# Attention key blocks paired 1 with 2 and 0 with 3, values cast once, and the channel spectra copied on VectorE

## The chip, the cores and the metric

The kernel runs on one core of one Trainium2 chip. The metric is the device time of one execution in microseconds (us); lower is better. The core has a TensorE for matmuls (PE in the profile, with its weight loads as PEld), VectorE (DVE), ScalarE (ACT), GpSimd (POOL) and SyncE (SP). SP and POOL issue the DMAs here, and 16 DMA engines carry them out. SBUF has 128 rows (partitions). PSUM takes the matmuls' results in banks of 512 fp32 numbers a row.

## The reference

Two stages follow each other: attention with a sliding window of 128 keys and a linear distance bias, then a spectral mixing layer over its output.

```python
# q, k, v: (8 batches, 8 heads, 576 tokens, 64)
scores = scale * np.matmul(q, k.transpose(0, 1, 3, 2))
rel = pos[:, None] - pos[None, :]
bias = slopes[:, None, None] * (-np.abs(rel))[None, :, :]
mask = (rel >= 0) & (rel < window)            # window = 128
scores = np.where(mask, scores + bias[None], -1000000000.0)
attn = softmax(scores)                         # over keys
x = np.matmul(attn, v)                         # -> (8, 576, 512)
...
X = np.fft.rfft(x, axis=1)                     # the first 64 modes are kept
Yr = einsum('bmd,mde->bme', Xr, w_r) - einsum('bmd,mde->bme', Xi, w_i)
Yi = einsum('bmd,mde->bme', Xr, w_i) + einsum('bmd,mde->bme', Xi, w_r)
y = np.fft.irfft(Y, n=S, axis=1)
u = x + y
return u + np.maximum(u @ w_ch, 0.0)
```

The inputs are fp32: q, k and v are 9.4 MB each, w_r and w_i have 64 matrices of 512 x 512 each (67 MB each), and w_ch is 1 MB. The output is (8, 576, 512) in fp32.

## The kernel before

Attention works in 16 units, a unit being one batch and four heads. A unit's four heads are two head pairs (e = 0, 1) times two positions h. The 576 tokens are four full blocks of 128 (`FULL = 4`) and a tail of 64 (`TAIL`). Because the window is 128 keys, a block of keys only meets the queries of its own block and of the next.

The scores are computed transposed, keys on the rows. One score tile `sc` holds two key blocks: 64 rows (even or odd keys, the index j) of one block in rows 0 to 63 and 64 rows of the other in rows 64 to 127. Before the change, `pair` 0 is blocks 0 and 1 and `pair` 1 is blocks 2 and 3. There are four score tiles in a unit, t = 2 * pair + h. ScalarE turns each into `att` with an exponential (`exp`, L307). For pair 0 the bias and the window are applied behind it by a multiplication with a table on VectorE (`mask`, L318); for pair 1 they are added in PSUM ahead of the scores, as a matmul with the identity (L284).

`value` multiplies `att` with the values. Each row group of 64 has its own copy place in `vb`: the values of the lower rows stand in the left W = 66 columns, those of the upper rows in the right 66, and the rest is zero. So one matmul over all 128 rows writes 132 columns, two query tiles at once. The two columns beyond the 64 of the head hold ones, which gives the softmax sums. The tail's values are in a tile of their own, `vt`. `norm` divides by the sums (L359 and L360) and writes x in bf16. `cast` brings q, k and v from fp32 to bf16 on VectorE (for v in two instructions of 64 rows, L246, and one for the tail, L248), and then issues the load of the unit two further on, as the raw buffers are double.

For each batch, `spectrum` transforms x to 64 modes on TensorE (L381), and `channels` copies the result from PSUM into XC with two ScalarE instructions (L402 and L403), the second with the opposite sign. For the last batch the work is halved between ScalarE and VectorE. The result of `spectrum` is in the same PSUM place (tag tp) as the transposes of k and q.

The order of the work is written by hand: the list `STAGE` says for each stage which step of which unit is issued, and every engine carries out its instructions in that order. The loads of q, k and v go through SP's queue (L232, L212, L225), those of v for the last two units through POOL's. The weights of the mixing layer are loaded by POOL with a conversion to bf16 (`load_w`, L472). In attention they are paced: a small copy (`gate`, L565) waits for the k cast of two units ahead, and behind it one weight matrix is loaded. Behind attention come packs of two matrices (`load_packs`, L491), and TensorE multiplies each matrix with the spectra as it lands (L886). A last part computes the output from the spectra and x (L842) and stores it.

Of the kernel before, what the change touches and what calls it, by code (L numbers as in the profile page):

```python
# [20 lines left out]
P = 128  # L21
D = 64
# [8 lines left out]
TPP = 9  # L31

W = D + 2

NC = 24

# [70 lines left out]
class _Attention:  # L107


    def __init__(self, tc, ctx, q, k, v, consts, x, XC, raw):  # L110
        self.tc, self.nc = tc, tc.nc
        self.q, self.k, self.v = q, k, v
        self.ident, self.F, self.FT = consts
        self.x, self.XC = x, XC
        B, H, S, _ = q.shape
        self.S, self.NG = S, H // 4
        self.units = [(b, g) for b in range(B) for g in range(self.NG)]
        self.raw = raw
        end = ctx.enter_context(tc.tile_pool(name="aend", bufs=1))
        self.sums = ctx.enter_context(tc.tile_pool(name="asum", bufs=2))  # L120
        self.mid = ctx.enter_context(tc.tile_pool(name="amid", bufs=2))
        self.ps = ctx.enter_context(tc.tile_pool(name="aps", bufs=1, space=PSUM))
        fix = ctx.enter_context(tc.tile_pool(name="afix", bufs=1))
        self.table = fix.tile([P, H, 2, 2 * P], BF16, name="mask")
        self.bias = fix.tile([P, H, 2, 2 * P], BF16, name="bias")
        self.qkT = [fix.tile([P, 2, 2, (FULL + 1) * P], BF16, name=f"qkT{i}") for i in range(2)]
        at = (fix, end)
        self.att = [at[i].tile([P, FULL * 8 * P + 64], BF16, name=f"att{i}") for i in range(2)]
        self.vb = [at[i].tile([P, 2, 4, 2, 2 * W], BF16, name=f"vb{i}") for i in range(2)]
        self.vt = [end.tile([P, 4, 2, W], BF16, name=f"vt{i}") for i in range(2)]  # L130
        self.loaded, self.casted, self.open = {}, {}, {}

    def fixtures(self, i):
        nc = self.nc
        for t, tail in ((self.vb[i], self.vt[i]),):
            for half in range(2):
                row = slice(64 * half, 64 * half + 64)
                c0 = W * half
                nc.gpsimd.memset(t[row, :, :, :, W - c0 : 2 * W - c0], 0.0)
                nc.gpsimd.memset(t[row, :, :, :, c0 + D : c0 + W], 1.0)  # L140
            nc.gpsimd.memset(tail, 0.0)
            nc.gpsimd.memset(tail[64:96, :, :, D:], 1.0)
        nc.gpsimd.memset(self.att[i][:, FULL * 8 * P :], 1.0)

    def distances(self, pool):

        nc = self.nc
        key_i = pool.tile([P, 2, 2], I32)
        for half in range(2):
            nc.gpsimd.iota(key_i[64 * half : 64 * half + 64], [[1, 2], [-P, 2]], base=0,  # L150
                           channel_multiplier=2)
        key = pool.tile([P, 2, 2], FP32)
        nc.gpsimd.tensor_copy(key, key_i)
        self.near = [pool.tile([P, 2, 2 * P], BF16) for _ in range(2)]

        def window(out, half, c0, width, n):
            row = slice(64 * half, 64 * half + 64)
            sign = 1 - 2 * n
            nc.gpsimd.affine_select(
                out=out[row, :, c0 : c0 + width],  # L160
                in_=key[row, :, n].unsqueeze(-1).broadcast_to([64, 2, width]),
                compare_op=ALU.is_ge, fill=-float(2**20), base=-n,
                pattern=[[-sign, 2], [sign, width]], channel_multiplier=-2 * sign,
            )

        for half in range(2):
            for n in range(2):
                window(self.near[0], half, n * P, P, n)
        nc.gpsimd.tensor_copy(self.near[1][:64], self.near[0][:64])
        nc.gpsimd.tensor_copy(self.near[1][64:, :, : P + TAIL], self.near[0][64:, :, : P + TAIL])  # L170
        window(self.near[1], 1, P + TAIL, TAIL, 0)

    def slope(self, h):
        return 2.0 ** (-8.0 * (h + 1) / self.table.shape[1])
# [26 lines left out]
    def load(self, w, u):  # L201
# [5 lines left out]
        if w == "v":  # L207
            t = self.raw[w][:, u % 2]
            sv = self.v[b, hs]
            if u < len(self.units) - 2:  # L210
                for h in range(4):
                    nc.sync.dma_start(  # L212
                        out=t[:, :2, h],
                        in_=sv[h, : FULL * P].rearrange("(r p j) d -> p r (j d)", r=2, j=2),
                    )
                queue = nc.sync
            else:
                for r in range(2):
                    nc.gpsimd.dma_start(
                        out=t[:, r],  # L220
                        in_=sv[:, 2 * r * P : 2 * (r + 1) * P].rearrange(
                            "h (p j) d -> p h (j d)", j=2),
                    )
                queue = nc.gpsimd
            queue.dma_start(  # L225
                out=t[64:96, 2],
                in_=sv[:, FULL * P :].rearrange("h (p j) d -> p h (j d)", j=2),
# [10 lines left out]
    def cast(self, u, w):  # L238

        nc = self.nc  # L240
        src = self.loaded.pop((w, u))
        if w == "v":
            src = src.rearrange("p s h (j d) -> p s h j d", j=2)
            for half in range(2):
                row = slice(64 * half, 64 * half + 64)
                nc.vector.tensor_copy(  # L246
                    self.vb[u % 2][row, :, :, :, W * half : W * half + D], src[row, :2])
            nc.vector.tensor_copy(self.vt[u % 2][64:96, :, :, :D], src[64:96, 2])  # L248
        else:
            dst = self.mid.tile([P, TPP, 2, D], BF16, tag=w, name=w)  # L250
            nc.vector.tensor_copy(dst.rearrange("p j e d -> p e j d"), src)
            self.casted[u, w] = dst
        self.load(w, u + 2)
# [20 lines left out]
    def score(self, u, t):  # L274
# [12 lines left out]
                )  # L287
        for j in range(2):
            for half in range(2):
                blk = 2 * pair + half  # L290
                spans = [(blk * P, 0, min(2 * P, self.S - blk * P))]
                if blk == FULL - 1:
                    spans.append((FULL * P, 192, TAIL))
                for k0, c0, n in spans:
                    for e in range(2):
                        row = slice(64 * e, 64 * e + 64)
                        nc.tensor.matmul(  # L297
                            sc[64 * half : 64 * half + 64, e, j * 256 + c0 : j * 256 + c0 + n],
                            lhsT=qkT[row, 1, h, k0 + j : k0 + P : 2],
                            rhs=qkT[row, 0, h, k0 : k0 + n],  # L300
                            start=not biased, stop=True, skip_group_check=biased,
                        )
        self.open[t, u] = sc
# [16 lines left out]
    def value(self, u, e):  # L320
# [1 line left out]

        nc = self.nc
        b, g = self.units[u]
        odd = b % 2
        att, vb, vt = self.att[u % 2], self.vb[u % 2], self.vt[u % 2]
        last = u == len(self.units) - 1 and e == 1
        av = self.ps.tile([P, 2, 512], FP32, tag="sc" if last else "av", bufs=2 if last else 1)
        for h in range(2):
            bank = av[:, h, : (FULL + 1) * W]  # L330
            todo = []
            for pair in range(2):
                rhs = [vb[:, pair, 2 * e + h, j] for j in range(2)]
                todo.append((pair, 0, 2 * pair, rhs))
                if pair == 1 and odd:
                    todo.append((pair, P, 3, [r[:, :W] for r in rhs]))
                    todo.append((pair, P - 64, 4, [r[:, W:] for r in rhs]))
                else:
                    todo.append((pair, P, 2 * pair + 1, rhs))
            todo.append((1, 192 - 64 * odd, 4, [vt[:, 2 * e + h, j] for j in range(2)]))  # L340
            for n, (pair, c0, qt, rhs) in enumerate(todo):
                for j in range(2):
                    o = (((2 * pair + h) * 2 + e) * 2 + j) * 256 + c0
                    nc.tensor.matmul(  # L344
                        bank[:, qt * W : qt * W + rhs[j].shape[1]],
                        lhsT=att[:, o : o + P], rhs=rhs[j],
                        start=(n == 0 and j == 0), stop=(n == len(todo) - 1 and j == 1),
                        skip_group_check=True,
                    )
        self.open["av", e, u] = av  # L350

    def norm(self, u, e):
# [2 lines left out]
        av = self.open.pop(("av", e, u))  # L355
        cs = slice((4 * g + 2 * e) * D, (4 * g + 2 * e + 2) * D)
        rec = self.sums.tile([P, 2, FULL + 1], FP32, tag="rec", name="rec")
        tiles = av[:, :, : (FULL + 1) * W].rearrange("p h (t n) -> p h t n", n=W)
        nc.vector.reciprocal(rec, tiles[:, :, :, D])  # L359
        nc.vector.tensor_tensor(  # L360
            out=self.x[:, b, :, cs].rearrange("p t (h d) -> p h t d", h=2),
# [28 lines left out]
    def channels(self, u, _):  # L390
# [8 lines left out]
            "p (q s t b m) -> p q t s b m", q=2, s=3, t=2, b=8)[:, :, :, :, b]  # L399
        if u < len(self.units) - 1:  # L400
            src = xt[:, 0].rearrange("p (q t) r m -> p q t r m", q=2)
            nc.scalar.copy(view[:, :, :, 1:], src)  # L402
            nc.scalar.mul(view[:, :, :, 0], src[:, :, :, 1], -1.0)  # L403
        else:
            lo, hi = slice(0, 2), slice(2, 4)
            nc.scalar.copy(view[:, 0, :, 1:], xt[:, 0, lo])
# [622 lines left out]
```

## Time and profile before

| | |
|---|---|
| median of the runs | 438.14 us (438.12 to 438.55, 3 runs) |
| the profiled execution | 437.99 us, of which the span of the profile is 436.1 us |
| granted TensorE clock, mean | 0.862 |
| busy in the span | PE 316.2, PEld 177.7, DVE 184.5, ACT 162.3, POOL 90.2 us |
| read from HBM, written to it | 162.53 MB, 9.44 MB |
| moved by the DMA engines | 105.54 MB, mean 242 GB/s |

How to read the profile: the page gives the busy time of each engine, then the span in 40 slices (a digit is tenths of the slice, PEclk the granted TensorE clock in tenths). "DMA share" is the time that packets were under way against 16 engines; it passes 1 where packets overlap on an engine. GB/s counts what is written: a weight that is read in fp32 and written in bf16 counts with half of what is read. The chain of waits is the work that ended last, followed back from the last instruction. A group of instructions has line, engine, operation, tiles and shapes, count, busy time and mean, and then the idle time before it with what ended it. A wait has the engine and line that waited, what it waited for, and the total, the number and the longest, in us.

### The profile page before, as it was taken

Reading aid. Unit: us, or ns where it says so; the run is one execution under the profiler, and the core shown is the slowest. Engines: PE = TensorE matmul, PEld = TensorE weight load, DVE = VectorE, ACT = ScalarE, POOL = GpSimd, SP = SyncE. Lnnn points to the kernel's source line nnn. Section 1 sums busy time; section 2 is a strip of 40 time slices with the busy share of each in tenths; the row PEclk is TensorE's granted clock in tenths of the full one; section 3 lists DMA queues with packets and bytes.
Section 4 is the critical chain, followed back from the end, with each engine's and each line's share of the span. In section 5 each row is a group of like instructions: output and inputs, shape, how many; then the busy total and the mean of one; then the engine's idle time right before and its main releaser. Section 6 shows DMA issues by size and latency. Waiting matters only on the chain.

```text
span 436.1 us, 8292 instructions
## 1 busy us (share of the span) xinstructions
PE 316.2 (73%) x3488; PEld 177.7 (41%) x3509; DVE 184.5 (42%) x332; ACT 162.3 (37%) x211; POOL 90.2 (21%) x170
## 2 busy tenths in 40 slices
PE   5589899979686635543442487999889999788982
PEld 4367677757565312111111133444434444334430
DVE  7789799887783301000000021322213233122684
ACT  6949899988681000000000011322222322102780
POOL 8701010103424002222112110101111110012600
PEclk9969999999999955555555569999999999989997
DMA  8999999999999999999999999999999999998598
GB/s 285 326 311 310 290 316 300 307 298 299 252 217 212 215 215 213 214 214 214 215 212 214 214 215 214 215 214 215 215 214 214 215 215 215 213 215 153 190 378 311
DMA packets 50453, 105.54 MB, mean 242 GB/s; under 512 B 4032, under 2 KB 21072, under 8 KB 50416
## 3 DMA queue, kind: packets, MB, share of 16 engines
q0 software_dynamic: 19440, 68.41, 77.9%
q1 hardware_dynamic: 30976, 36.60, 25.3%
q8 instruction: 27, 0.44, 0.4%
q14 instruction: 10, 0.08, 0.1%
HBM read 162.53 MB, written 9.44 MB: 394 GB/s over the span
## 4 chain that ended last, share of the span: by engine, by line
DMA 71%; PE 10%; DVE 8%; issue 5%; POOL 2%; ACT 1%; SPq 1%; DVEq 0%; POOLq 0%; ACTq 0%
DMA w<-in_moe_w_i_dram 42%; DMA wch<-in_moe_w_ch_dram 8%; DMA qr<-in_q_dram 7%; DMA vr<-in_v_dram 6%; DVE o L842 3%; DMA qr<-in_moe_w_i_dram 3%; PE my L702 2%; DMA vr<-in_moe_w_r_dram 2%; DMA kr<-in_k_dram 2%; DVE vb L246 1%; PE acc L886 1%; PE av L344 1%; POOL Z L648 1%; PE my L659 1%; DVE att L318 1%
## 5 line engine op out<-in xcount | busy, mean ns | idle before, releaser
L886 PE MATMUL acc<-w,XC 128*32 128x512 bf16 x456 | 80.3, 478 | 68.5 <-DMA w<-in_moe_w_i_dram 34.2
L886 PEld LDWEIGHTS <-XC 128*32 128x32 bf16 x508 | 38.4, 147 | 109.2 <-issue 82.8
L307 ACT ACTIVATE att<-sc 128x1024 bf16<-128x1024 f32 x64 | 64.1, 1032 | 9.7 <-PE sc L297 9.6
L636 ACT CAST ZW<-zw 128x512 bf16<-128x512 f32 x8 | 4.7, 585 | 142.9 <-PE zw L634 142.9
L344 PE MATMUL av<-vb,att 128*128 128x132 bf16 (+1 forms) x576 | 38.4, 217 | 13.3 <-DVE x L360 8.6
L344 PEld LDWEIGHTS <-att 128*128 128x128 bf16 x704 | 36.6, 98 | 18.7 <-DVE x L360 12.0
L608 DVE TENSOR_SCALAR yq<-acc 128x512 bf16<-128x512 f32 x14 | 9.6, 687 | 81.8 <-PE acc L886 81.8
L702 PE MATMUL my<-wch,xT 128*64 128x512 bf16 x288 | 34.5, 381 | 5.7 <-ACT x L733 4.2
L711 ACT CAST XW<-my 128x512 bf16<-128x512 f32 x36 | 19.3, 589 | 50.5 <-PE my L659 50.5
L683 DVE COPY xT<-tr 128x1024 bf16<-128x1024 bf16 x18 | 12.4, 692 | 54.9 <-PE tr L681 54.9
L269 ACT COPY qkT<-tp 128x1152 bf16<-128x1152 bf16 x30 | 33.5, 1116 | 4.1 <-PE tp L263 3.6
L491 POOL DMA_DIRECT2D w<-in_moe_w_r_dram x22 | 15.6, 710 | 72.1 <-PE acc L886 46.1
L491 POOL DMA_DIRECT2D w<-in_moe_w_i_dram x23 | 16.3, 709 | 64.1 <-PE acc L886 45.3
L297 PE MATMUL sc<-qkT 64*64 64x256 bf16 (+2 forms) x640 | 25.1, 263 | 4.8 <-ACT qkT L269 1.2
L360 DVE TENSOR_TENSOR x<-av,rec 128x640 bf16<-128x640 f32 x32 | 26.4, 825 | 1.1
L702 PEld LDWEIGHTS <-xT 128*64 128x64 bf16 x288 | 17.1, 109 | 21.5 <-issue 9.1
L246 DVE CAST vb<-vr 64x1024 bf16<-64x1024 f32 x32 | 22.6, 708 | 0.2
L733 ACT CAST x<-my 128x512 bf16<-128x512 f32 x18 | 10.5, 585 | 31.6 <-PE my L659 31.6
L297 PEld LDWEIGHTS <-qkT 64*64 64x64 bf16 x640 | 14.5, 109 | 19.1 <-issue 16.0
L734 DVE CAST x<-my 128x512 bf16<-128x512 f32 x18 | 12.4, 692 | 21.7 <-PE my L659 21.7
L842 DVE TENSOR_TENSOR o<-yy,r 128x1024 f32<-128x1024 f32 (+1 forms) x20 | 20.3, 1059 | 2.1 <-ACT r L802 1.9
L318 DVE TENSOR_TENSOR att<-att,mask 128x1024 bf16<-128x1024 bf16 x32 | 20.5, 682 | 0.0
(137 smaller groups left out, 424.7 us busy)
## 6 DMA issues: line engine op xcount, KB each, us to landing
w<-in_moe_w_i_dram POOLq DMA_DIRECT2D x23, 1024.0 KB, 36.2
w<-in_moe_w_r_dram POOLq DMA_DIRECT2D x22, 1024.0 KB, 35.6
qr<-in_q_dram SPq DMA_DIRECT2D x16, 576.0 KB, 7.9
kr<-in_k_dram SPq DMA_DIRECT2D x16, 576.0 KB, 7.9
w<-in_moe_w_r_dram POOLq DMA_DIRECT2D x16, 512.0 KB, 14.2
vr<-in_v_dram SPq DMA_DIRECT2D x56, 128.0 KB, 7.6
w<-in_moe_w_i_dram POOLq DMA_DIRECT2D x13, 512.0 KB, 24.0
out_dram<-o SPq DMA_DIRECT2D x13, 512.0 KB, 5.0
```

The lines of the kernel that those rows point to most:

```text
L246: nc.vector.tensor_copy(self.vb[u % 2][row, :, :, :, W * half : W * half + D], src[row, :2])
L269: (self.nc.vector.tensor_copy if u < 2 and w == "q" else self.nc.scalar.copy)(dst.rearrange("q h (p j) -> q h p j", j=TPP), tp.rearrange(" ...
L297: nc.tensor.matmul(sc[64 * half : 64 * half + 64, e, j * 256 + c0 : j * 256 + c0 + n], lhsT=qkT[row, 1, h, k0 + j : k0 + P : 2], rhs=qkT[r ...
L307: self.nc.scalar.activation(self.att[u % 2][:, kt * 8 * P : (kt + 1) * 8 * P], sc.rearrange("p e n -> p (e n)"), AF.Exp, scale=1.0 / math. ...
L318: nc.vector.tensor_tensor(out=rows, in0=rows, in1=self.table[:, heads], op=ALU.mult)
L344: nc.tensor.matmul(bank[:, qt * W : qt * W + rhs[j].shape[1]], lhsT=att[:, o : o + P], rhs=rhs[j], start=(n == 0 and j == 0), stop=(n == l ...
L360: nc.vector.tensor_tensor(out=self.x[:, b, :, cs].rearrange("p t (h d) -> p h t d", h=2), in0=tiles[:, :, :, :D], in1=rec.unsqueeze(-1).br ...
L491: nc.gpsimd.dma_start(out=t.rearrange("p s a e -> p s (a e)"), in_=w[kinds.pop()][m : m + 2].rearrange("m (p a) e -> p m (a e)", a=4))
L702: nc.tensor.matmul(mm[ROWS[half]], lhsT=lhsT, rhs=wch[:, dt], start=(dt == 0), stop=False, skip_group_check=True,)
L711: nc.scalar.copy(XW[:, j, n], mms[n])
L842: nc.vector.tensor_tensor(out=o[:, c], in0=yy[:, c], in1=r[:, c], op=ALU.add)
L886: nc.tensor.matmul(into[32 * (m % 4) : 32 * (m % 4) + 32], lhsT=XC[:, c0 : c0 + 31 * NM + 1 : NM], rhs=wq[t][a], start=(ri == 0 and a == 0 ...
```

## The change

Three things change.

- The key blocks are paired (1, 2) and (0, 3) (`BLOCKS`) instead of (0, 1) and (2, 3). For pair 0 the columns of the upper block are put in another order, so that the two blocks' shares of query tile 2 stand in the same columns. The tables of distances are built accordingly.
- `vb` holds the values once, without zeros beside them, and `cast` fills it with one instruction over 128 rows. `load` brings v in the new order: blocks 1 and 2 with two DMAs over 128 rows, block 0 with one DMA over rows 0 to 63, block 3 with one DMA over rows 64 to 127, and the tail as before. In the last two units the same five go through POOL's queue, where three did. `value` has matmuls over 64 rows with 66 columns each, alternating between lower and upper rows, for all but query tile 2, which still takes 128 rows; the results stand in slots of 172 columns, and query tiles 0 to 2 and 3 to 4 are in different PSUM banks.
- `channels` uses VectorE instead of ScalarE for all batches but the last. Its place in `STAGE` is the same.

```diff
+SLOT = 172
+BLOCKS = ((1, 2), (0, 3))
...
-        self.vb = [at[i].tile([P, 2, 4, 2, 2 * W], BF16, name=f"vb{i}") for i in range(2)]
+        self.vb = [at[i].tile([P, 2, 4, 2, W], BF16, name=f"vb{i}") for i in range(2)]
...
-        for t, tail in ((self.vb[i], self.vt[i]),):
-            for half in range(2):
-                ...
-                nc.gpsimd.memset(t[row, :, :, :, W - c0 : 2 * W - c0], 0.0)
-                nc.gpsimd.memset(t[row, :, :, :, c0 + D : c0 + W], 1.0)
-            nc.gpsimd.memset(tail, 0.0)
-            nc.gpsimd.memset(tail[64:96, :, :, D:], 1.0)
+        nc.gpsimd.memset(self.vb[i][:, :, :, :, D:], 1.0)
+        nc.gpsimd.memset(self.vt[i], 0.0)
+        nc.gpsimd.memset(self.vt[i][64:96, :, :, D:], 1.0)
...
-            if u < len(self.units) - 2:
-                for h in range(4):
-                    nc.sync.dma_start(
-                        out=t[:, :2, h],
-                        in_=sv[h, : FULL * P].rearrange("(r p j) d -> p r (j d)", r=2, j=2),
+            queue = nc.sync if u < len(self.units) - 2 else nc.gpsimd
+            for rows, r, first in ((slice(0, P), 0, 1), (slice(0, 64), 1, 0), (slice(64, P), 1, 3)):
+                for hh in (slice(0, 2), slice(2, 4)) if r == 0 else (slice(0, 4),):
+                    n = 2 * (rows.stop - rows.start)
+                    queue.dma_start(
+                        out=t[rows, r, hh],
+                        in_=sv[hh, first * P : first * P + n].rearrange("h (p j) d -> p h (j d)", j=2),
                     )
-                queue = nc.sync
-            else:
-                for r in range(2):
-                    nc.gpsimd.dma_start(
-                        ...
-                queue = nc.gpsimd
...
-            for half in range(2):
-                row = slice(64 * half, 64 * half + 64)
-                nc.vector.tensor_copy(
-                    self.vb[u % 2][row, :, :, :, W * half : W * half + D], src[row, :2])
+            nc.vector.tensor_copy(self.vb[u % 2][:, :, :, :, :D], src[:, :2])
...
         for j in range(2):
             for half in range(2):
-                blk = 2 * pair + half
-                spans = [(blk * P, 0, min(2 * P, self.S - blk * P))]
-                if blk == FULL - 1:
-                    spans.append((FULL * P, 192, TAIL))
-                for k0, c0, n in spans:
+                k0, c0 = BLOCKS[pair][half] * P, 2 * P * j
+                spans = [(k0, k0, c0, min(2 * P, self.S - k0))]
+                if biased and half:
+                    spans.append((FULL * P, FULL * P, c0 + 3 * TAIL, TAIL))
+                elif half and j == 0:
+                    spans = [(k0, k0, P, 2 * P)]
+                elif half:
+                    spans = [(k0, k0, 3 * P, P), (k0, k0 + P, 0, P)]
+                for k0, q0, c0, n in spans:
...
+        for j in range(2):
+            c0 = 2 * P * j
+            todo += [(low, 1, 0, c0, vb, j), (high, 0, 3, 2 * P - c0, vb, j),
+                     (low, 1, 1, c0 + P, vb, j), (high, 1, 3, c0, vb, j),
+                     (low, 0, 1, c0, vb, j), (high, 1, 4, c0 + P - back, vb, j)]
+            far += [(slice(0, P), 0, 2, c0 + P, vb, j), (high, 1, 4, c0 + 3 * TAIL - back, vt, j)]
+        started = set()
+        for row, pair, qt, c0, src, j in todo + far:
+            for h in range(2):
+                vals = src[row, pair, 2 * e + h, j] if src is vb else src[row, 2 * e + h, j]
+                o, d = ((2 * pair + h) * 2 + e) * 4 * P + c0, qt * SLOT + h * W
+                nc.tensor.matmul(
+                    flat[:, d : d + W], lhsT=att[row, o : o + P], rhs=vals,
+                    start=(qt > 2) not in started, stop=True, skip_group_check=True,
+                )
+                started.add(qt > 2)
...
-            nc.scalar.copy(view[:, :, :, 1:], src)
-            nc.scalar.mul(view[:, :, :, 0], src[:, :, :, 1], -1.0)
+            nc.vector.tensor_copy(view[:, :, :, 1:], src)
+            nc.vector.tensor_scalar_mul(view[:, :, :, 0], src[:, :, :, 1], -1.0)
```

## The prediction

> **What bounds the kernel now.** I read the page's slices and its queue table first, then the table by stages, the chain, the groups and waits of the attention stage, and last the DMA issues. The page's throttle and DMA rows, one digit per 10.9 us:
>
> ```profile
> PEclk9969999999999955555555569999999999989997
> DMA  8999999999999999999999999999999999998598
> GB/s 285 326 311 310 290 316 300 307 298 299 252 217 212 215 215 213 214 214 214 215 212 214 214 215 214 215 214 215 215 214 214 215 215 215 213 215 153 190 378 311
> ```
>
> The DMA engines are at 9 in every slice from the second to the 36th, in attention (up to about 139 us) as in the weight stream. The table by stages (the two last columns are DMA share and GB/s) says it finer:
>
> ```profile
> 20.00:40.00 20.00, 15.45 (x243) 12.16 (x246) 16.87 (x31) 13.75 (x15) 1.38 (x4) 0.83 1.08 307
> 60.00:80.00 20.00, 18.43 (x356) 14.46 (x358) 18.46 (x33) 18.88 (x21) 2.42 (x6) 1.00 1.08 304
> 80.00:100.00 20.00, 15.77 (x295) 12.64 (x287) 16.94 (x30) 16.55 (x20) 2.11 (x6) 1.00 1.08 296
> 120.00:140.00 20.00, 14.96 (x267) 12.04 (x266) 12.87 (x26) 10.67 (x14) 6.17 (x10) 1.00 1.06 215
> 180.00:380.00 200.00, 143.06 (x1045) 63.49 (x1044) 39.54 (x78) 32.21 (x58) 31.99 (x51) 0.81 1.07 214
> 397.00:436.00 39.00, 27.90 (x308) 12.26 (x310) 23.16 (x27) 19.98 (x27) 9.76 (x19) 0.94 0.78 264
> ```
>
> A share of 1.06 to 1.08 is full: the pure weight stream shows 1.07. I counted the trace's DMA packets in flight against 16 engines: from 10 to 390 us the idle room sums to 0.2 us. PE, DVE and ACT are at 80 to 95% in attention, but they wait for loads, and the chain says the same:
>
> ```profile
> DMA 71%; PE 10%; DVE 8%; issue 5%; POOL 2%; ACT 1%; SPq 1%; DVEq 0%; POOLq 0%; ACTq 0%
> ```
> ```profile
> DVE q L251 <- DMA qr<-in_q_dram: 6.8, 6, 1.6
> DVE k L251 <- DMA kr<-in_k_dram: 2.0, 1, 2.0
> POOL vr L219 <- DVE vb L246: 10.3, 2, 5.6
> ACT XC L402 <- PE xt L381: 6.0, 6, 2.3
> ```
>
> So the program is 397 us of DMA work in a fixed amount, plus a tail of 39 us that the change doesn't touch. An engine saving in attention moves no byte sooner; only a change of DMA work, or a gap in it, moves the end.
>
> **The change, part by part.** Measured groups of the attention stage:
>
> ```profile
> L246 DVE CAST vb<-vr 64x1024 bf16<-64x1024 f32 x32 | 22.6, 708 | 0.2
> L344 PE MATMUL av<-vb,att 128*128 128x132 bf16 x448 | 36.2, 224 | 13.3 <-DVE x L360 8.6 <-DVE att L318 4.1
> L402 ACT CAST XC<-xt 128x512 bf16<-128x512 f32 x7 | 4.1, 585 | 6.0 <-PE xt L381 6.0
> L403 ACT ACTIVATE XC<-xt 128x256 bf16<-128x256 f32 x7 | 2.7, 390 | 0.0
> ```
>
> *Value cast.* Two casts of 64 rows become one of 128 rows with the same 1024 elements per row; the nearest 128-row form, q and k with 1152, takes 0.77 to 0.80, so about 0.70. DVE saves 0.7 us a unit, 11 us over 16 units, beside full DMA: 0 on the path.
>
> *Spectra copies.* ACT loses 7 x (0.585 + 0.390) = 6.8 us. DVE gains 7 x (0.687, L608's 128x512 from PSUM, + 0.426, L408's 128x256) = 7.8 us. On DVE they stand behind the v cast and ahead of the k cast, the first norm, the q cast, both masks and the second norm. In the stage at 66 us the second norm ended at 66.9, PE then did values and spectrum until 69.3; the shortened v cast would end near 68.0, so DVE stalls some 1.4 us there. Who waits: PE's k transpose (it shares the tp bank), the loads that the k and q casts release, and value 1 behind the first norm. Every second unit DVE is longer by 1.4 + 1.1 - 0.7 = 1.8 us, the other shorter by 0.7. Two units without DMA waits took 7.2 + 6.3 = 13.4 us (second norms at 52.7, 59.8, 66.1), the DMA-paced ones 15.5 (80.0, 95.6, 111.1). 13.4 + 1.8 - 0.7 = 14.5 still fits under 15.5, so 0; a q load takes 7.9 us from issue to landing, against some 1.5 for its bytes at 390 GB/s, so the queue holds about 6 us that cover a late cast.
>
> *Values and scores on PE.* Now 20 or 24 matmuls a call, 1.18 and 1.24 us in the chain; starts lie 58 ns apart for 132 columns and 29.5 for 66. Then 32 of 66: 0.94 us one after another, about 0.59 if the 24 half-row ones run two abreast. Between 128-row and 64x64 tiles the trace leaves about 0.1 us (50.67 to 50.77), and a call now changes form four times: 1.0 to 1.35 us, against 1.2. Scores gain 64 short matmuls over the kernel, a few us of PE at most. Covered as above.
>
> *POOL and start.* Four large memsets (0.97 to 1.43) go and small ones and window selects (0.3 to 0.5) come; DMA is full from 4 us on, so 0. In the last two units POOL issues five v loads for three, 2 x 0.76 us more each, ahead of the gate and weight loads queued behind. DMA's one thin spot is there, at 118 to 118.6 us (0.12 us of room). I take 0; bound 0 to 1.5 us.
>
> *The v loads themselves.* This is the only edit that touches the full resource.
>
> ```profile
> vr<-in_v_dram SPq DMA_DIRECT2D x56, 128.0 KB, 7.6
> vr<-in_v_dram SPq DMA_DIRECT2D x14, 64.0 KB, 7.4
> ```
>
> A unit keeps five issues, the same bytes and 512-byte packets, but two of the 128 KB issues now write 64 rows each instead of 128: 512 of 1152 packets. No 64-row load exists before; the nearest is the 32-row tail (64 KB). From the packet records: the last 128 packets of a unit's v (mostly the tail) took 33.06 ns on average, the 1024 before 29.46. Excess 3.6 ns x 512 / 16 engines = 0.115 us a unit. In the table by stages, q and k alone move at 392 GB/s, and the stretch just behind a tail drops:
>
> ```profile
> 10.30:11.30 1.00, 0.08 (x1) 0.08 (x2) 0.86 (x1) 1.00 (x2) 0.89 (x3) 1.00 1.08 241
> 11.50:13.50 2.00, 1.98 (x18) 0.92 (x16) 1.10 (x1) 0.96 (x2) 1.84 (x5) 1.00 1.05 392
> ```
>
> 1 us x (1 - 241/392) = 0.385 us lost in the shadow of one narrow issue, if the tail causes it. Lower bound: packets fall to the 27 ns most of them show, 2.46 ns x 1024 x 14 / 16 = 2.2 us gained. Upper: each of the two narrow issues costs 0.385: 0.77 x 14 = 10.8 us. I take 0.2 us a unit, between 0.115 and 0.385 (their geometric mean is 0.21), since issues for low and high rows follow each other and engines drift apart by about 0.4 us, so that both halves are written at once in part. 16 x 0.2 = 3.2 us, all on the path, as DMA never idles.
>
> *Sum.* Profiled execution 437.99 us = span 436.1 + 1.9 outside it; it stands 0.15 under the median 438.14. Changes on the path: 3.2 + 0. Forecast 438.1 + 3.2 = 441.3 us.
>
> **Rivals.**
> 1. *Nothing moves.* Narrow loads cost no more than wide ones, the rest is hidden. For: in units 4 to 8 the tail's packets took 27 to 30 ns. Against: 34 to 42 in units 0 to 2 and 9 to 13. 438.1 us.
> 2. *Not slower but faster: the engines set attention's pace.* DVE is at 18.46 of 20 from 60 to 80; if loads only look full because they are issued early, DVE's net 11 - 7.8 = 3.2 us comes off: 434.9. It decides if the units' period falls under 7.6 us. Against: bytes are fixed and the room for more is 0.2 us. The cheaper packets above (2.2 us, 435.9) would end on this side too.
> 3. *The order on DVE and PE opens gaps in DMA.* If PE's form changes and the stall on the spectrum add 2 us a pair to the 14.5, it passes 15.5 by 1: over the five or so pairs up to 111 us, 5 us on top of the 3.2: 446. For: PE is at 18.43 of 20. It decides from 15.5 us a pair.
> 4. *Narrow loads run at half rate.* Alone, v moved at 305 GB/s (8.5 to 10 us). 262 KB a unit at half of that costs 0.86 us more: 13.8 us in 16 units, 452. For: the 241 GB/s. Against: the tail's packets are nowhere twice as long on average. [...]
>
> **How the numbers follow.** Forecast case 0.50, rival 1 0.17, rival 2 0.16, rival 3 0.10, rival 4 0.07. A measurement of this kernel tells about 0.2% (0.9 us) from no change. Faster 0.16, same 0.17, slower 0.67. The slower cases' own range is 439 to 449 (the 10.8 us bound). The whole range reaches down into rival 2, to 436.2, leaving out some 0.10 below and 0.08 above 449.
>
> **What would show it.** DMA share stays at 1.05 or more to about 400 us; the weight stream's last chunk lands some 3 us later; the tail stays 39 us; DVE's cast group halves to 16 of 0.70; XC moves to DVE with a wait on the spectrum of about 1.4 us; 512-byte packets grow past 29.5 ns on average. Wrong if those packets are no longer (rivals 1, 2), or if DMA's share falls under 1 in attention (rival 3).

## The result and the profile after

The changed kernel takes 456.52 us in the median (454.05 to 461.58, 6 runs), against 438.35 us before (437.88 to 443.18, 6 runs of the same session). The ratio is 1.0384, with a 95% interval of 1.0325 to 1.0443; it leaves out the runs of either kernel that were disturbed. The forecast was 441.3 us: right in sign, 15 us short, and outside its range.

The profiled execution took 461.58 us (span 459.7), the longest of the six. The slices of its page, 11.5 us each:

```profile
PEclk9859898978975969555555558999999999989998
DMA  8999999999997999999999999999999999999498
GB/s 269 278 289 263 277 253 262 268 259 252 254 202 152 188 215 213 215 213 215 213 215 212 215 213 216 214 214 215 214 215 214 215 214 215 214 214 177 148 378 309
```

The DMA engines are still busy in nearly every slice, but in attention they move 252 to 289 GB/s where they moved 285 to 326. The table by stages (the last three columns are granted clock, DMA share and GB/s) puts numbers to it:

```profile
60.00:80.00 20.00, 17.45 (x328) 12.55 (x329) 14.32 (x27) 14.45 (x15) 1.41 (x4) 0.91 1.10 260
80.00:100.00 20.00, 16.03 (x339) 11.58 (x343) 15.91 (x30) 14.06 (x16) 2.41 (x6) 0.94 1.09 259
120.00:140.00 20.00, 11.41 (x193) 8.28 (x195) 8.99 (x17) 8.89 (x9) 8.24 (x16) 0.80 0.88 195
180.00:380.00 200.00, 132.72 (x939) 58.26 (x941) 35.60 (x74) 26.65 (x48) 33.72 (x53) 0.76 1.07 214
420.50:459.70 39.20, 27.69 (x307) 12.07 (x309) 23.17 (x26) 19.84 (x27) 9.80 (x19) 0.95 0.76 260
```

Share 1.10 with 260 GB/s, against 1.08 with 304: the engines are as full as before and each packet takes longer. The weight stream is unchanged (214 GB/s), and the last part is as long as before (39.2 us against 39.0), only its start came 23.5 us later (420.5 against 397). The loss lies in the attention stage. The granted clock is 0.91 from 60 to 80 us where it was 1.00; that is not the cause, as e2 below moves only 261 GB/s from 40 to 60 us at a clock of 1.00. The chain of the whole span (its DMA share is 71% as before) and the waits from 20 to 165 us agree that loads are waited for:

```profile
DMA 71%; PE 16%; DVE 6%; issue 2%; POOL 2%; ACT 1%; SPq 1%; DVEq 0%; POOLq 0%; ACTq 0%
```
```profile
DVE q L245 <- DMA qr<-in_q_dram: 11.5, 6, 3.6
DVE k L245 <- DMA kr<-in_k_dram: 10.6, 6, 3.7
POOL vr L218 <- DVE vb L241: 12.5, 2, 8.0
DVE XC L399 <- PE xt L378: 8.8, 6, 1.6
```

VectorE waited 8.8 us for q and k loads before, and 22.1 now. The issues of the page (KB of each, median us from issue to landing) were at 7.9 us for q and k and 7.6 us for v before:

```profile
qr<-in_q_dram SPq DMA_DIRECT2D x16, 576.0 KB, 9.4
kr<-in_k_dram SPq DMA_DIRECT2D x16, 576.0 KB, 10.3
vr<-in_v_dram SPq DMA_DIRECT2D x56, 128.0 KB, 9.3
```

The instructions themselves came out as worked out (cast 0.70 us, copies 0.687 and 0.426):

```profile
L241 DVE CAST vb<-vr 128x1024 bf16<-128x1024 f32 x16 | 11.0, 685 | 3.7 <-DMA vr<-in_v_dram 3.7
L399 DVE CAST XC<-xt 128x512 bf16<-128x512 f32 x7 | 4.8, 692 | 8.8 <-PE xt L378 8.8
L400 DVE TENSOR_SCALAR XC<-xt 128x256 bf16<-128x256 f32 x7 | 2.9, 415 | 0.0
```

The packet records of SP's queue hold the whole difference. The 512-byte packets (v) grew from 29.9 to 38.4 ns on average, which over 16 engines is 30.1 to 38.7 us; the 2304-byte packets (q and k), which the change doesn't touch, from 104.7 to 124.0 ns, 53.6 to 63.5 us. Together that is 18.5 us of DMA time, beside 18.2 us between the medians; with 4.8 us more of idle DMA room, told next, it makes 23.3 of the 23.6 us by which this span is longer. A profile of e15 below, which has the same loads (457.24 us), shows 39.6 and 123.3 ns: 19.3 us more DMA time in a span that is 19.4 us longer.

This profile has a second loss: 5.0 us of idle DMA room between 130 and 170 us, where the share falls to 0.88. The chain there, in start, us and what:

```profile
122.10 15.83 DMA kr<-in_k_dram
137.93 0.03 issue
137.96 0.02 DVEq L245
137.98 0.04 issue
138.02 0.76 DVE k L245
```

GpSimd's gate waits for that k cast (it runs at 138.91 us, the next weight load is issued at 139.38), and attention's own loads have run out. From 10 to 390 us the profiles of two other kernels with the same shapes of loads (e15 and e17 below, 457.24 and 453.0 us) have 0.3 and 0.2 us of such room, so this seems to belong to the spread between 454 and 462 rather than to the median.

### The profile page after: what moved, and what is told of

It is laid out like the page before. It is cut to its first block, busy times and chain, and to the rows that moved or that the text cites. A ratio compares the mean times of both kernels' runs of the same rounds, so it can differ in the third digit from the quotient of the medians.

```text
span 459.7 us, 9045 instructions
## 1 busy us (share of the span) xinstructions
PE 330.9 (72%) x3872; PEld 181.8 (40%) x3893; DVE 179.9 (39%) x330; ACT 157.6 (34%) x197; POOL 85.9 (19%) x170
## 4 chain that ended last, share of the span: by engine, by line
DMA 71%; PE 16%; DVE 6%; issue 2%; POOL 2%; ACT 1%; SPq 1%; DVEq 0%; POOLq 0%; ACTq 0%
DMA w<-in_moe_w_i_dram 34%; DMA vr<-in_v_dram 9%; DMA wch<-in_moe_w_ch_dram 8%; DMA w<-in_moe_w_r_dram 7%; DMA kr<-in_k_dram 6%; DMA qr<-in_q_dram 6%; PE av L341 4%; DVE o L839 2%; PE my L699 2%; PE acc L883 2%; PE tp L257 1%; PE sc L295 1%; DMA out_dram<-o 1%; PE sc L278 1%; POOL Z L645 1%
## 5 line engine op out<-in xcount | busy, mean ns | idle before, releaser
L883 PE MATMUL acc<-w,XC 128*32 128x512 bf16 x456 | 78.8, 477 | 64.3 <-DMA w<-in_moe_w_r_dram 32.1
L341 PE MATMUL av<-vb,att 64*128 64x66 bf16 (+1 forms) x896 | 35.0, 206 | 24.5 <-DVE x L357 15.8
L341 PEld LDWEIGHTS <-att 64*128 64x128 bf16 (+1 forms) x1024 | 31.8, 102 | 37.3 <-issue 9.6
L708 ACT CAST XW<-my 128x512 bf16<-128x512 f32 x36 | 19.3, 589 | 50.7 <-PE my L656 50.7
L295 PE MATMUL sc<-qkT 64*64 64x256 bf16 (+3 forms) x704 | 28.1, 277 | 6.1 <-issue 2.9
L488 POOL DMA_DIRECT2D w<-in_moe_w_r_dram x22 | 15.5, 704 | 68.8 <-PE acc L883 45.3
L295 PEld LDWEIGHTS <-qkT 64*64 64x64 bf16 x704 | 18.5, 118 | 23.5 <-issue 20.4
L562 POOL COPY gate<-k 1x1 bf16<-1x1 bf16 x13 | 2.3, 177 | 95.2 <-DVE rec L356 70.1
```

What stands on the lines that cost most here:

```text
L295: nc.tensor.matmul(sc[64 * half : 64 * half + 64, e, c0 : c0 + n], lhsT=qkT[row, 1, h, k0 + j : k0 + P : 2], rhs=qkT[row, 0, h, q0 : q0 + ...
L341: nc.tensor.matmul(flat[:, d : d + W], lhsT=att[row, o : o + P], rhs=vals, start=(qt > 2) not in started, stop=True, skip_group_check=True,)
L488: nc.gpsimd.dma_start(out=t.rearrange("p s a e -> p s (a e)"), in_=w[kinds.pop()][m : m + 2].rearrange("m (p a) e -> p m (a e)", a=4))
L708: nc.scalar.copy(XW[:, j, n], mms[n])
L883: nc.tensor.matmul(into[32 * (m % 4) : 32 * (m % 4) + 32], lhsT=XC[:, c0 : c0 + 31 * NM + 1 : NM], rhs=wq[t][a], start=(ri == 0 and a == 0 ...
```

## The experiments

Times are medians; each is beside 438.3 to 438.9 us of the kernel before on the same chip.

**Wide loads in the changed kernel, 64-row loads in the kernel before.** Two runs exchange the loads and leave all else; in e1 the second slot then holds blocks 2 and 3 in place of 0 and 3.

```diff
 e1: after
-for rows, r, first in ((slice(0, P), 0, 1), (slice(0, 64), 1, 0), (slice(64, P), 1, 3)):
+for rows, r, first in ((slice(0, P), 0, 1), (slice(0, P), 1, 2)):
...
 e2: before
+for r, p0, p1, heads in ((0, 0, P, 2), (1, 0, 64, 4), (1, 64, P, 4)):
```

> The changed kernel with one edit: the v values of the second pair of key blocks are loaded with two DMAs over all 128 rows (two heads each, tokens 256 to 511) in place of one DMA over rows 0 to 63 and one over rows 64 to 127. So block 2's values stand where block 0's should; bytes, packets and the number of issues stay. Theory L (the two half-row loads cost the time, all else is hidden beside DMA): 438 us, within 436.5 to 440. Theory E (the order on the engines costs it: VectorE's stall on the spectrum, TensorE's form changes and its half-clock windows): 452 us or more, as the engines' work is untouched.

> The kernel before with only the v loads changed: blocks 0 and 1 with two DMAs over 128 rows, block 2 with one over rows 0 to 63, block 3 with one over rows 64 to 127, the tail as before; the last two units the same through POOL's queue. All engines' work stays as before. Theory L: 452 to 458 us, 14 to 20 more than before, and the share of time of the SP queue's packets near the changed kernel's 28.1%. Theory E: 437.5 to 439, as no engine's work changes.

Measured: 441.69 us, ratio 1.0089 (1.0072 to 1.0106), and 453.4 us, ratio 1.0352 (1.0326 to 1.0378). The loads alone cost 15.0 us in the old kernel; taking them out of the new one gives 14.8 us back. The packets of e2 have nearly the changed kernel's lengths (37.4 and 123.1 ns), those of e1 the old ones (30.0 and 103.6). Some 3 us were left.

**Which rows.** The same 64 rows by a load that crosses row 64, and a kernel without most tails.

```diff
 e3: before
+(1, 0, 32, 4), (1, 32, 96, 4), (1, 96, P, 4)
 e4: before
+if u < 2:
     queue.dma_start(out=t[64:96, 2], ...)
```

> As the half-row loads in the kernel before, but blocks 2 and 3 are cut at other rows: one DMA over rows 32 to 95 (128 KB), one over rows 0 to 31 and one over rows 96 to 127 (64 KB each). Theory L1 (what counts is whether a DMA's rows lie on one side of row 64): the 64-row DMA across the middle is free and only half as many bytes are one-sided: half of the half-row loads' extra, 444 to 448 us. Theory L2 (what counts is how few rows a DMA has): three loads of 64 rows or fewer in place of two cost at least as much as the half-row loads: 454 us or more.

> The kernel before without the tail's v load (32 rows, 64 KB, rows 64 to 95) from unit 2 on; the tail's values stay those of units 0 and 1. 14 loads fewer. Theory L says that this one-sided load too casts a shadow: its bytes at 392 GB/s (0.17 us) and 0.2 to 0.385 us of shadow, 14 times: 5 to 8 us less, 430 to 433. If a narrow load costs only its bytes: 2.3 to 3.4 us less, 434.7 to 436.

Measured: 447.76 us (1.0193 to 1.0261) and 435.57 us (0.9927 to 0.9959). With half of the rows in a crossing load, 9.4 of the 15.0 us remain. The tail is worth 2.8 us, 0.2 us each, hardly more than its bytes at 392 GB/s (0.17 us); the shadow of 0.385 us that the prediction took as its upper bound for one narrow issue was too much for a tail, and too little for the new loads (15.0 us for 32 of them in e2, 0.47 us each).

**One load over both halves, and turns.** If a load that writes one half only is dear, one that writes both should be cheap. e5 takes blocks 0 and 3 in one load for each head, by a stride; e6 is e5 with the copies on ScalarE; e8 keeps 64-row loads, but one head at a time, low and high in turns.

```diff
 e5
+out=t[:, 1, hh], in_=sv[hh, : FULL * P].rearrange("(k p j) d -> k p (j d)", k=4, j=2)[0:4:3]
 e8
+tuple((1, p0, p0 + 64, h, h + 1) for h in range(4) for p0 in (0, 64))
```

> The changed kernel with all its data right, but the values of blocks 0 and 3 come in four DMAs, one for each head, that each write all 128 rows (64 rows from block 0, 64 from block 3, by a stride in DRAM) in place of two that write 64 rows each. Theory 'one side': what costs is that a DMA writes only rows of one half, so this is like the run with wide loads: 441.7 us (440 to 443.5). Rival 'source': the two separate stretches of DRAM cost by themselves: 450 us or more.

> As the strided one, and the two channel copies of each spectrum are ScalarE's again. Some 3.4 us of the slowdown is still open once the loads are wide. Theory 'channels': the copies on VectorE delay the casts that free the raw buffers, and so open the gaps on the DMAs: 438.4 us (437.3 to 439.5). Rival 'pairing': the scores and value products in the new pairing do it (more and narrower TensorE calls, at the half clock in places): 441 to 442.5 us, as with the copies on VectorE.

> The changed kernel, but its two 64-row loads are cut into eight, one for each head and half, issued in turns: low half, high half, low half and so on. The bytes, packets and rows are the same, six issues more for each unit on the queue. Theory 'order in time': what costs is that all 16 DMA engines write the same half for some microseconds, so turns of 64 packets help: 443 to 449 us. Rival 'shape': a DMA of 64 rows is dear by itself, whatever is beside it: 455 to 459 us.

Measured: 529.75 us (1.2041 to 1.2103), 529.94 us (1.2035 to 1.21) and 481.34 us (1.0933 to 1.0995), far above every price named; e5's rival, "450 us or more", is met by the number alone, since another thing was at work. The packets were short again (30.3 ns in e5, 29.6 in e8), but there were too few of them at a time. First the queue of SP in e5 (start, us, what), then two stages by their table, of e5 and of e8:

```profile
70.58 6.71 SPq L223 DMA_DIRECT2D vr<-in_v_dram  x4
77.41 3.02 SPq L228 DMA_DIRECT2D vr<-in_v_dram  x1
```
```profile
74.00:76.00 2.00, 0.70 (x28) 0.60 (x28) 1.97 (x5) 0.51 (x1) 0.70 (x2) 1.00 0.19 55
```
```profile
70.00:72.00 2.00, 1.79 (x38) 1.21 (x38) 1.91 (x5) 1.72 (x2) 0.71 (x2) 0.50 0.24 53
```

In e5 some 2.3 of SP's packets are in flight on average from 74.5 to 78.5 us, and the tail's issue behind the strided loads takes 3.02 us. Why so few of a strided load's packets are in flight is not shown. In e8 an issue takes 0.60 us for 64 packets of 30 ns, so on average 64 x 30 / 600 = 3.2 are in flight. Neither tells what full engines would do, and e6 can't speak on the copies, as nothing else mattered in it.

**The copies alone.** The kernel before with them on VectorE:

```diff
-nc.scalar.copy(view[:, :, :, 1:], src)
-nc.scalar.mul(view[:, :, :, 0], src[:, :, :, 1], -1.0)
+nc.vector.tensor_copy(view[:, :, :, 1:], src)
+nc.vector.tensor_scalar_mul(view[:, :, :, 0], src[:, :, :, 1], -1.0)
```

> The kernel before with the channel copies alone moved to VectorE. Theory 'channels': 440.5 to 442.5 us. Rival 'pairing': 437.8 to 439.2 us, no change that can be measured.

Measured: 440.31 us, ratio 1.0036 (1.0017 to 1.0055): 1.7 us, where the prediction had 0. The DMA's idle room from 10 to 390 us is 1.0 us in place of 0.2, most of it between 50 and 70 us. The table and the waits of e7:

```profile
60.00:80.00 20.00, 17.31 (x327) 13.52 (x322) 18.80 (x34) 16.44 (x18) 2.19 (x5) 1.00 1.04 283
```
```profile
DVE XC L402 <- PE xt L381: 4.4, 6, 0.9
PE tp L263 <- DVE XC L403: 2.0, 6, 0.3
```

VectorE is at 18.80 of 20 us there, and the share falls from 1.08 to 1.04. Its waits for q and k loads from 20 to 120 us fall from 8.8 to 1.8 us: the loads are now there before VectorE is.

**Two queues.** The high half's load goes to ScalarE's queue.

```diff
+(nc.scalar if first == 3 and u < len(self.units) - 2 else queue).dma_start(
```

> The changed kernel, all as it is, but of the two 64-row loads of each unit the one for the high half is issued by ScalarE to a queue of its own (units 0 to 13), so that both halves can be written at the same time. In the run with turns for each head the 512-byte packets were back at 29.6 ns, but the queue then ran dry between short issues. Theory 'one half at a time': with two queues the packets mix without more issues, 512-byte packets at 30 to 33 ns, and the time is 440.5 to 445 us. Rival 'two queues are no cover': the halves still come one after the other, or ScalarE's exponentials wait behind the issue: 450 us or more.

Measured: 451.53 us (1.029 to 1.0335), 5 us less than the changed kernel in the medians. Packets of the new queue took 39.3 ns. In units 6, 7, 11, 12 and 13 the two loads ran side by side, with 962 packets of the high half and 1210 of the low half; these took 44.6 and 45.6 ns on average (31 to 54 by unit). In the other units one load was largely through before the other began. The table of unit 12, while both ran:

```profile
110.60:112.20 1.60, 1.60 (x55) 1.34 (x53) 1.49 (x3) 0.86 (x1) 0.00 (x0) 1.00 1.23 227
```

Some six packets of each half are in flight there on average, of 18.7 in all, and they take 44.8 and 46.2 ns. So writing both halves at the same moment, by two loads, does not bring back the 30 ns of wide loads, and the theory that two queues would mend it fails by its packets as by its time.

**What is left with wide loads.** e10 is e1 with the copies on ScalarE. e11 is e1 with GpSimd's v loads in two issues and the tail. e12 gets the new pairing with wide loads: the cast moves the halves, in four instructions of 64 rows.

```diff
 e12
+for rows, r, first in ((slice(0, P), 0, 0), (slice(0, P), 1, 2)):
...
+nc.vector.tensor_copy(vals[lo, 0], src[hi, 0])
+nc.vector.tensor_copy(vals[hi, 0], src[lo, 1])
+nc.vector.tensor_copy(vals[lo, 1], src[lo, 0])
+nc.vector.tensor_copy(vals[hi, 1], src[hi, 1])
```

> The run with wide loads (441.7 us; slot 1 holds the values of blocks 2 and 3 in place of 0 and 3) with the channel copies on ScalarE again. The copies alone cost the kernel before 1.7 us. If the costs add: 440.0 us (439.2 to 440.8), and 1.7 us are left for the pairing. If the copies only cost in the kernel before and the rest is the pairing's: 441 to 442. If all of the rest came by VectorE's queue, 438 to 439.

> The run with wide loads (441.7 us), and the values of the last two units come again in two issues of 256 KB and the tail on GpSimd's queue, as in the kernel before, in place of four and the tail; the copies stay on VectorE. Theory 'handover': the two further issues of 0.72 us for each of two units delay the weight loads behind them in that queue, and open the gap at 119 to 122 us: 439.5 to 440.8 us. Rival: those issues lie beside running transfers: 441.2 to 442.2 us.

> The changed pairing with right data and only wide loads: tokens 0 to 255 and 256 to 511 by 128 rows each, and the cast moves the halves to their blocks, in four instructions of 64 rows by 512 elements (an estimate of 0.37 us each from 0.69 us for 1024 elements, so 0.8 us more on VectorE for a unit than the one cast); copies on ScalarE, last two units in two issues as before. If loads, copies and GpSimd's issues are all that cost: 438 to 439.5 us, the same as before. If the pairing itself costs what is left: 439.5 to 441. Below 437.5 only if the narrower TensorE calls free buffers earlier than before.

Measured: 438.49 us (0.9988 to 1.0023), 441.7 us (1.0063 to 1.0128) and 440.0 us (1.0019 to 1.0053). With wide loads and the copies on ScalarE, the whole rest (one cast, the new scores and value products, GpSimd's fixtures and issues) makes no difference that can be measured. The copies are worth 3.2 us there, more than the 1.7 alone. GpSimd's two further issues are worth nothing. e12 is 1.6 us slower than before; what sets it apart from e10 on the engines is its longer casts (VectorE is busy for 188.1 us, in e10 for 172.2), which were not tested alone. The stage of e10 looks as before the change, its clock too:

```profile
60.00:80.00 20.00, 18.56 (x413) 13.50 (x414) 16.96 (x30) 18.64 (x21) 2.41 (x6) 1.00 1.08 307
```

The idle room of the DMAs sets the slower of these kernels apart, by their profiled executions: 0.2 us before (437.99) and 0.4 in e10 (437.69), against 1.0 in e7 (440.29), 1.4 in e1 (439.74), 1.3 in e11 (440.81) and 1.6 in e12 (440.03). It doesn't order these four, and it is less than the time they lose.

**Turns of two heads, and the copies in the changed kernel.** e13 cuts the 64-row loads into four, so that the queue doesn't run dry; e14 adds the copies on ScalarE; e15 is the changed kernel with nothing but the copies back on ScalarE.

```diff
 e13, e14
+tuple((1, p0, p0 + 64, h, h + 2) for h in (0, 2) for p0 in (0, 64))
```

> The changed kernel, its two 64-row loads cut into four of two heads each, in turns (low, high, low, high). Issues on the queue for a unit are an estimated 2 x 0.46 + 4 x 0.60 + 0.55 + 2 x 0.38 = 4.6 us of the 6.5 us that a unit takes, so the queue should not run dry as it did with turns of one head. Theory 'one half at a stretch': 512-byte packets near 30 to 34 ns, 441.5 to 448 us. Rival 'shape': packets near 38 ns as in the changed kernel, 454 to 459 us.

> As the turns of two heads, and the channel copies on ScalarE again: 3 us below that run if the copies cost here what they cost with wide loads; the same as that run if slow transfers hide them.

> The changed kernel with nothing but the channel copies back on ScalarE. If the parts add: 453.4 us (452.5 to 454.5), as the kernel before with the 64-row loads alone. If the slower transfers give VectorE the time for the copies: 455.5 to 457.5 us, as the changed kernel.

Measured: 457.79 us (1.0415 to 1.0462), 458.12 us (1.0407 to 1.0475) and 456.49 us (1.0379 to 1.0437). Turns bring nothing: the packets of the 64-row loads take 39 and 47 ns, as in e2. And the copies cost nothing that shows in the changed kernel: its slower loads leave VectorE the time (14.32 us busy from 60 to 80 us, against 18.80 in e7).

**Shape or side, and the DRAM stretches.** e18 keeps shape, bytes and issues of e2, but both 64-row loads write rows 32 to 95. e16 gives the kernel before the very loads of the changed one, e17 the changed one those of e2.

```diff
 e18: before
+low, high = ((0, 64), (64, P)) if u < 2 else ((32, 96), (32, 96))
+for r, (p0, p1), heads, first in ((0, (0, P), 2, 0), (1, low, 4, 2 * P), (1, high, 4, 3 * P)):
```

> The kernel before with two loads of 64 rows by four heads for slot 1, as in the run that gave 453.4 us, but from unit 2 on both loads write rows 32 to 95 (32 on each side of row 64); rows 0 to 31 and 96 to 127 of slot 1 keep the values of units 0 and 1. Shape, bytes, packets and issues are the same. Theory 'one half': 438 to 441 us. Rival 'shape': 452 to 455 us.

> The kernel before with exactly the value loads of the changed kernel: slot 0 holds tokens 128 to 383, slot 1 blocks 0 and 3 (so the values are those of other tokens than its products want); pairing, casts and copies as before. If the stretches of DRAM are worth the 3 us: 456 to 457.5 us. If the pairing is: 452.5 to 454.5 us.

> The changed kernel, its loads of the same shapes but from the other stretches: slot 0 tokens 0 to 255, slot 1 blocks 2 and 3 (values of other tokens than its products want). If the stretches are worth 3 us: 453 to 454.5 us. If the pairing is: 455.5 to 457.5 us.

Measured: 473.83 us (1.0782 to 1.084), 453.72 us (1.0289 to 1.0379) and 457.34 us. The last is the median of 453.0, 454.27, 460.4 and 462.97; its interval, 1.0316 to 1.0365, goes by the first two. The time of e18 tells nothing of the rows: both loads write the same rows, so the second waits until the first has landed, and SP stands still in each unit:

```profile
SPq L214 <- DMA vr<-in_v_dram: 69.4, 15, 8.3
```

Its packets do tell. Mean ns of a unit's v packets in the order of the queue, units 3 to 13 (in e13, each of the two middle columns is one turn of low and one of high rows):

| | wide, 512 | first 64-row, 256 | second 64-row, 256 | tail, 128 |
|---|---|---|---|---|
| before (all wide) | 28.7 | 29.6 | 29.6 | 31.8 |
| after | 30.9 | 40.7 | 44.6 | 48.4 |
| e2, rows 0-63 and 64-127 | 28.9 | 38.7 | 46.4 | 46.2 |
| e13, turns of two heads | 28.2 | 39.5 | 47.3 | 42.5 |
| e18, rows 32-95 twice | 27.7 | 29.5 | 27.8 | 28.2 |

The queue's waits empty the engines at times in e18, but not always. The table of e18 while such a load ran with full engines, ahead of that of the changed kernel while its loads for one half ran:

```profile
71.50:72.00 0.50, 0.45 (x8) 0.45 (x9) 0.00 (x0) 0.50 (x1) 0.00 (x0) 1.00 1.05 295
```
```profile
60.50:63.50 3.00, 2.52 (x43) 2.02 (x43) 1.72 (x4) 1.74 (x2) 0.00 (x0) 1.00 1.15 208
```

From 71.5 to 72.0 us 256 packets, just one such load, took 28 ns on average. In the other window the 512-byte packets took 48 to 57 ns, and the 2304-byte packets beside them 164 to 204 (means of each half us). So it is the side, by the packets: a load of 64 rows on both sides of row 64 (29.5 and 27.8 ns in e18) is as fast as one of 128 (28.7 and 29.6 before), a load of 64 rows on one side is not (38.7 and 46.4 in e2). e3 agrees by its time: 447.76 us with half of the rows in a crossing load, 453.4 with none (e2). Why the side of row 64 counts is not shown, nor what holds the packets at 45 ns when two loads, one for each half, run side by side (e9).

## Why the prediction was right or wrong

- **What bounds the kernel**: right. The DMAs bound attention in both kernels, and the end moved by what they lost. Of the signs named, the casts of 0.69 us, the wait of about 1.5 us for the spectrum, the longer packets and the last part of 39 us came; but the last part began 23.5 us later in the profiled run, where the sign for the weights said 3. The engines' "80 to 95%" was loosely read (ScalarE is at 13.75 of 20 us, 69%, from 20 to 40 us), and nothing hung on it.
- **"I take 0.2 us a unit" for the v loads**: this is the step that failed. It measured 15.0 / 16 = 0.94 us a unit in the kernel before (e2), near rival 4's 0.86, to which I gave 0.07. (The sum counted 16 units, its bounds the 14 of SP's queue.) Three parts of that step were wrong. The tail was the nearest row, and its 31.8 to 33 ns did not carry over: the same tail takes 48.4 ns behind two one-sided loads and 28.2 behind two crossing ones (e18). A load of 128 packets says little about 640 in a row. Second, the sum counted the packets of the new loads alone; of the 18.5 us of packet time, 9.9 are in the q and k packets beside and behind them. Third, "both halves are written at once in part", since loads for low and high rows follow each other, gave no relief: in turns of 64 KB the packets stay at 39 to 47 ns (e13), and side by side from two queues at 45 (e9).
- **The argument against rival 4**, that the tail's packets are nowhere twice as long, was of the same kind and fell with it. Rival 4 came near by luck in part: the one-sided packets took 41 and 45 ns for 30, not twice as long, and more than half of the loss is in q and k, which it left out.
- **Value cast, values and scores, fixtures, GpSimd's issues at 0**: right (e10, e11).
- **Copies at 0**: wrong where the loads are wide (1.7 us in e7, 3.2 between e10 and e1), right in the changed kernel (e15). "14.5 still fits under 15.5" compared means of the period; e7 shows idle DMA room all the same, 0.8 us of it between 50 and 70 us. Which late cast lets it in was not separated.
- **Rival 3, gaps in the DMAs**: in part, 5.0 us in the profiled run, little in others.
- **Open**: with the copies on ScalarE, 64-row loads cost 18.0 us in the new pairing (e10 to e15) and 15.0 in the old one (before to e2); the intervals of e15 and e2 just fail to overlap. Neither the pairing nor the stretches of DRAM is shown to be the reason. The old pairing stays at 453.7 us with the changed kernel's stretches (e16). The changed kernel with e2's stretches (e17) had two runs in the range expected if the stretches are the reason (453.0 and 454.27 us), and two above the range for the pairing (460.4 and 462.97). The profile of the first has 98.0 us of DMA time in the q, k and v packets of SP's queue, near e16's 99.2 and e2's 100.7, where e15 has 103.0.

No version here that keeps all the loads beats the kernel before: e10, whose second slot holds block 2 where the products want block 0, equals it, and e12, with all values in their places, is 1.6 us slower.

## What to carry to other kernels

When the DMAs are full, cost a layout change by the rows that each load writes before you cost the engines: two loads of 64 rows, low and high, in place of two of 128 with the same bytes took 3.5% here (e2), while the saved cast and the rearranged matmuls moved nothing (e10). Neither turns between the halves (e13, 457.79 us) nor a second queue (e9, 451.53 us) cured it; wide loads whose halves the cast moves came within 1.6 us (e12). A short load of a kind at the end of a stream is a poor price for a long run of that kind (the tail's packets took 33 ns before the change, those of the new loads 41 and 45 ns), and the packets that share the engines with it must be in the sum (9.9 of the 18.5 us were theirs). An engine step that seems covered can still cost 0.4% (e7), it seems through the casts that release buffers, and cost nothing once something else is slower (e15).

## What the runs showed of the hardware that was not expected

- A load to rows of one half slows what runs beside and behind it: q and k packets went from 104.7 to 124.0 ns, and the mix moved 208 GB/s (60.5 to 63.5 us), where q, k and a wide v load move 370 (64.5 to 66.5 us of the same trace).
- Two loads for the two halves, side by side from two queues, had packets of 45 ns with full engines (e9, unit 12: 18.7 in flight, 227 GB/s); wide loads have 30.
- Turns of 64 KB between the halves in one queue (e13) did not raise the rate: its 64-row packets took 39 and 47 ns. Its q and k packets were back at 103.9 ns, but 6.9 us of idle DMA room came in their place, and the time stayed.
- Loads strided over two stretches ran with 2.3 packets in flight and held up the queue behind them (the tail's issue took 3.02 us): 91 us more than the kernel before (e5).
